# Halving the first batch's query side and writing out the order of every engine in a linear-attention and MLP kernel

## The chip, the core and the metric

The kernel runs on one core of a Trainium2 chip. The metric is device time in microseconds for one execution of the whole program. A core has five engines that run side by side, each through its own list of instructions: PE (matrix products; its weight loads are shown apart as PEld), DVE (vector engine), ACT (scalar engine, which evaluates functions such as exp from a table that has to be loaded), POOL (a second vector engine, which also issues the software DMA queue) and SP (which issues most DMAs). An engine never skips an instruction: one that waits holds up everything behind it on its list.

## What is computed

There are 8 batches, 8 heads, 576 tokens, head size 64 and 128 features. The attention output is the input of a layer norm and a two-layer MLP with a residual.

```python
def phi(x):
    proj = np.einsum('bhsd,df->bhsf', x, w_phi)
    proj = proj - np.max(np.abs(proj), axis=-1, keepdims=True)
    return np.concatenate([np.exp(proj), np.exp(-proj)], axis=-1)
q_p, k_p = (phi(q), phi(k))
kv = np.einsum('bhsf,bhsd->bhfd', k_p, v)
z = np.sum(k_p, axis=2)
num = np.einsum('bhsf,bhfd->bhsd', q_p, kv)
den = np.einsum('bhsf,bhf->bhs', q_p, z)[..., None] + 1e-06
x = num / den                                  # then (batch, token, 512)
mu = np.mean(x, axis=-1, keepdims=True)
var = np.mean((x - mu) ** 2, axis=-1, keepdims=True)
xn = (x - mu) / np.sqrt(var + 1e-06) * g_ln
out = x + np.maximum(xn @ w_ch1, 0.0) @ w_ch2  # 512 x 2048, 2048 x 512
```

## The kernel before

**Units.** Attention is cut into 32 units; a unit is two heads of one batch, 576 tokens each, so that units 0 to 3 are batch 0 and units 4 to 7 batch 1. Of a unit's tokens 512 per head are the main part and 64 the tail; the tails (`px`, L943 and L944) are handled apart. A unit goes through these steps: its q and k are transposed on PE (L829, `qkT_ps`) and copied out as bf16 (`qkT`, L844 on DVE or L846 on ACT). The function `a_main` multiplies by w_phi with tokens on the partitions (`pm`, L984 or L990) and DVE takes the largest absolute value of each token (`m`, L1047, one reduction of 128x1024 for k and one for q). For k, ACT takes the exponentials (`eb`, L1067), a small factor `ek` (L1056, L1060) is folded into v on POOL (`vv`, L1074 to L1080), and PE forms `kv` (L1135, L1141, in the PSUM tile `n_bank`), which is copied out as `KV` (L1149 on DVE, L1151 on ACT). For q, `a_tails` multiplies with features on the partitions (`pt`, L999) and ACT takes the exponentials (`ea`, L1111). `a_num` multiplies `ea` with `KV` on PE (`num`, L1199, L1205), DVE scales and adds the two halves (`numc`, L1221, L1227) and inverts the denominators (`rden`, L1233), and POOL writes the quotient into `x` (L1266, L1270). From unit 4 on, `pm` and `pt` of two units are multiplied together in one group on two halves of the array (`a_group`, 64 rows each).

**Token groups.** The MLP works on groups of four token tiles, 512 tokens. Group 0 is batch 0, so it needs units 0 to 3; group 1 is batch 1. For a group, DVE takes mean and variance (L1338, L1350), the centred `xc` is formed (L1360, L1364), PE transposes it (L1302, `xT_ps`), the copy `xT` (L1312 on DVE, L1314 on ACT) carries g_ln, and then come the two products: `first` (L1431, `hT_ps`, sixteen blocks of four matmuls with 512 columns, each followed by a relu, L1439 on DVE or L1441 on ACT) and `second` (L1463, `ch_ps`). The factor 1/sqrt(var) is applied behind the second product; it is made on ACT as exp(-0.5 ln(var)), with L1370 (Ln) and L1371 (Exp). The last groups use products with fewer multiplications (L1597, L1780 and around).

**Weights.** w_ch1 comes in two DMAs of 1 MB (`load_w1`, L769) and w_ch2 in two (`load_w2`, L787), all issued by POOL through its software queue. Units 8 and later hold their loads back until the second half of w_ch1 has come (`HOLD`).

**The order.** The class `Order` collects every operation with its possible engines, its estimated time, and what it reads and writes. Before the change its `run` is a list scheduler: at each moment an engine takes, among the operations that are ready by its plan, the one with the lowest rank, and ranks come from the tables `OFF`, `SLACK` and `GATE`. The plan fixes the order on each engine (and which engine takes an operation that two could do); the chip then runs these lists and waits on semaphores. Where the plan has PE idle before 75 us (`WARM`), it puts in filler matmuls (L2061 and L2064, `n_bank<-wz`, 128x120), whose result nothing uses.

**The function table of ACT.** Near the start the program calls `preload_act_table_set("natural_log_exp_and_others")` (L1966 before, L2064 after), an operation of ACT with 1.3 us in the plan. The built program shows an ACT_TABLE_LOAD for it, and one ahead of any function that the table then in place doesn't hold.

Of the kernel before, what the change touches and what calls it, by code (L numbers as in the profile page):

```python
# [17 lines left out]
def bcast(ap: bass.AP, dim: int, n: int) -> bass.AP:  # L18
# [7 lines left out]
RELU = -983.1  # L26
WARM = 75.0
COLD, FIRST = 5.6, 10
SLACK = ((0.22, 0.0, 0.0, 1.02), (0.35, 0.6, 1.6, 1.03), (0.22, -1.1, 0.0, 1.28))
HOLD = 1  # L30
SHUT = 0.6
X_DMA, QK_DMA, AHEAD = 1, 8, 3
TILED = 4
LAND, LAND_T, LAND_W, TURN, BARRIER = 2.8, 1.5, 3.0, 0.004, 0.4
MIXED, STUCK = 1.5, 0.3
GATE = (("v", 4), ("v", 5))
OFF = (
    {
        "load": 0.0, "trans": -17.5, "trans.copy": -150.8, "mixed": -0.8, "mixed.max": 0.0,
        "mixed.exp": 45.4, "mixed.fold": 0.0, "k": 7.2, "k.max": -94.2, "k.em": -91.5,  # L40
        "k.exp": -40.2, "en": 0.0, "vv": -43.0, "q": 0.0, "q.max": -8.5, "q.em": 72.1,
        "tails": 0.0, "tails.exp": 121.1, "kv": 56.5, "kv.copy": -218.0, "num0": 940.5,
        "num1": 72.3, "num.dve": -95.7, "g1": 0.0, "g2": 0.0, "g3": 0.0, "put": 7.1, "ln": 0.0,
        "w1": 0.0, "w2": 0.0, "ln.c": 0.0, "ln.t": 0.0, "moe": 0.0,
    },
    {
        "load": 0.0, "trans": 37.9, "trans.copy": 0.9, "mixed": 166.7, "mixed.max": -24.8,
        "mixed.exp": 88.7, "mixed.fold": 0.0, "k": 748.4, "k.max": 0.0, "k.em": -35.7,
        "k.exp": 0.0, "en": 0.0, "vv": -48.0, "q": 0.4, "q.max": -0.3, "q.em": 52.8,
        "tails": 1.6, "tails.exp": 1.2, "kv": 45.2, "kv.copy": 19.6, "num0": -19.2,  # L50
        "num1": 107.5, "num.dve": -989.1, "g1": 0.0, "g2": 0.0, "g3": 0.0, "put": 90.6,
        "ln": 172.1, "w1": 0.0, "w2": 0.0, "ln.c": 0.0, "ln.t": 0.0, "moe": 0.0,
    },
    {
        "load": 0.0, "trans": 94.3, "trans.copy": 0.0, "mixed": 266.0, "mixed.max": -21.1,
        "mixed.exp": -4.0, "mixed.fold": 0.0, "k": -132.9, "k.max": -50.9, "k.em": -145.0,
        "k.exp": -269.5, "en": 0.0, "vv": 0.1, "q": 66.0, "q.max": 2.0, "q.em": 33.6,
        "tails": -201.9, "tails.exp": 120.7, "kv": 8.8, "kv.copy": -27.9, "num0": 5.2,
        "num1": 2.7, "num.dve": 115.4, "g1": 0.0, "g2": 0.0, "g3": 0.0, "put": -58.0, "ln": 0.0,
        "w1": 0.0, "w2": 0.0, "ln.c": 0.0, "ln.t": 0.0, "moe": 0.0,  # L60
    },
    {
        "load": 0.0, "trans": 0.0, "trans.copy": -2.2, "mixed": 27.3, "mixed.max": -46.6,
        "mixed.exp": -1.8, "mixed.fold": 0.0, "k": 11.3, "k.max": -17.6, "k.em": -80.2,
        "k.exp": 0.7, "en": 0.0, "vv": 0.0, "q": -27.7, "q.max": 1.8, "q.em": 0.0,
        "tails": -47.7, "tails.exp": -6.1, "kv": 0.0, "kv.copy": 35.2, "num0": -1.3,
        "num1": 121.1, "num.dve": -1.6, "g1": 0.0, "g2": 0.0, "g3": 0.0, "put": -58.0,
        "ln": -535.9, "w1": 0.0, "w2": 0.0, "ln.c": 34.1, "ln.t": -36.5, "moe": 80.8,
    },
    {  # L70
        "load": 0.0, "trans": 5.5, "trans.copy": 63.5, "mixed": 47.2, "mixed.max": 0.0,
        "mixed.exp": 73.5, "mixed.fold": 0.0, "k": 0.0, "k.max": 0.4, "k.em": -87.0,
        "k.exp": -137.4, "en": 0.0, "vv": 7.8, "q": 0.0, "q.max": 36.3, "q.em": 78.3,
# [417 lines left out]
def kernel(  # L491
# [1612 lines left out]
```

## Time and profile before

| | us |
|---|---|
| median of 3 runs | 357.06 (356.84 to 357.75) |
| span of the profiled execution | 354.4 |
| median less span | 2.7 |
| PE busy | 345.6 (98%) |
| DVE busy | 304.8 (86%) |
| ACT busy | 258.5 (73%) |
| POOL busy | 189.3 (53%) |

The profiled execution's own time is not listed apart from its span; the difference of 2.7 us to the median of the runs is taken as what lies around the span. The page of the profile gives busy time for each engine, groups of instructions by line, and the chain that ended last. In a row of a group, the numbers behind the first bar are total busy us and mean ns of one instruction, and those behind the second bar are the idle time of the engine just ahead of them, with what ended it. In a row of a timeline or of the chain come start, length, engine, operation and count. The view by windows gives the busy time of each engine in a stretch with the number of instructions. Busy time counts overlapping instructions once, so that a mean duration is somewhat longer than what one instruction adds.

### The profile page before, as it was taken

What the parts mean: (1) busy time and instruction counts of PE and PEld (TensorE: products, weight loads), DVE (VectorE), ACT (ScalarE), POOL (GpSimd) and SP (SyncE); (2) the same over time, 40 slices, a digit from 0 to 9 for tenths busy, and PEclk for the clock granted to TensorE, in tenths of its full rate; (3) what the DMA queues carried; (4) which work ended last, traced back from release to release, by engine and by line L of the source; (5) the groups of instructions that cost most, each with busy time, mean ns of one, the idle gap of its engine ahead of it and who ended that gap; (6) DMA issues with size and microseconds to landing.
All of it is one profiled execution on the core that took longest, in us unless ns stands there. A gap on an engine that the chain in (4) does not pass through costs nothing.

```text
span 354.4 us, 9372 instructions
## 1 busy us (share of the span) xinstructions
PE 345.6 (98%) x3606; PEld 221.1 (62%) x3632; DVE 304.8 (86%) x664; ACT 258.5 (73%) x551; POOL 189.3 (53%) x245
## 2 busy tenths in 40 slices
PE   8998999999999999999999999999999999999995
PEld 8987955556554555455545455555555578578884
DVE  5699987899987888988979989897778799999983
ACT  4997988598997996979696975787697833656410
POOL 5499755799644873747478798355546420000000
PEclk9999999999999999999999999999999999999999
DMA  7999999899996888489729242851051005400053
GB/s 210 311 215 287 210 281 246 215 235 258 294 276 175 209 185 215 115 141 280 202 68 209 72 110 47 147 153 35 2 126 63 3 7 116 123 2 3 0 120 118
DMA packets 93676, 53.89 MB, mean 152 GB/s; under 512 B 61104, under 2 KB 88048, under 8 KB 93632
## 3 DMA queue, kind: packets, MB, share of 16 engines
q1 hardware_dynamic: 89392, 47.72, 56.5%
q0 software_dynamic: 3328, 4.49, 7.1%
q10 hardware_dynamic: 912, 1.08, 0.9%
q8 instruction: 28, 0.46, 0.5%
q14 instruction: 16, 0.13, 0.1%
HBM read 36.77 MB, written 9.44 MB: 130 GB/s over the span
## 4 chain that ended last, share of the span: by engine, by line
PE 88%; DVE 8%; ACT 2%; issue 1%; DVEq 0%; ACTq 0%
PE hT_ps L1431 29%; PE ch_ps L1463 22%; PE ch L1597 9%; PE n_bank L2064 4%; PE pm L990 4%; PE n_bank L1141 4%; PE sum L1780 4%; PE num L1199 3%; PE pt L999 2%; DVE m L1047 2%; PE n_bank L1135 1%; DVE numc L1221 1%; PE n_bank L1199 1%; DVE numc L1227 1%; PE n_bank L1205 1%
## 5 line engine op out<-in xcount | busy, mean ns | idle before, releaser
L1431 PE MATMUL hT_ps<-xT,w 128*128 128x512 bf16 x496 | 118.4, 379 | 0.0
L1463 PE MATMUL ch_ps<-w,hT 128*128 128x512 bf16 x362 | 88.9, 379 | 1.3 <-issue 0.3
L1047 DVE TENSOR_REDUCE m<-pm 128x8 f32<-128x1024 f32 x64 | 76.8, 1214 | 7.1 <-PE pm L990 6.5
L1074 POOL TENSOR_TENSOR vv<-v,ek 128x1024 bf16<-128x1024 f32 x32 | 61.1, 1910 | 33.0 <-issue 18.2
L1431 PEld LDWEIGHTS <-w 128*128 128x128 bf16 x496 | 44.2, 98 | 44.0 <-issue 0.8
L1067 ACT ACTIVATE eb<-pm 128x1024 bf16<-128x1024 f32 x64 | 64.5, 1036 | 2.4 <-DVE m L1047 2.3
L1111 ACT ACTIVATE ea<-pt 128x1024 bf16<-128x1024 f32 x64 | 63.8, 1029 | 3.0 <-PE pt L999 2.7
L1266 POOL TENSOR_TENSOR x<-numc,rden 128x128 bf16<-128x128 f32 (+1 forms) x64 | 38.9, 613 | 38.6 <-DVE rden L1233 37.4
L1441 ACT ACTIVATE hT<-hT_ps 128x512 bf16<-128x512 f32 x68 | 40.6, 597 | 24.1 <-PE hT_ps L1431 23.2
L1463 PEld LDWEIGHTS <-hT 128*128 128x128 bf16 x384 | 34.0, 98 | 34.4 <-issue 0.8
L1439 DVE TENSOR_SCALAR hT<-hT_ps 128x512 bf16<-128x512 f32 x56 | 38.5, 687 | 8.6 <-PE hT_ps L1431 8.1
L1199 PEld LDWEIGHTS <-ea 128*128 128x128 bf16 x512 | 24.6, 97 | 10.5 <-issue 1.7
L1141 PE MATMUL n_bank<-vv,eb 128*128 128x65 bf16 x512 | 26.6, 194 | 0.0
L902 POOL TENSOR_TENSOR b<-qk,one 128x1024 bf16<-128x1024 f32 x11 | 20.9, 1896 | 8.9 <-DMA qkT<-b 5.5
L2064 PE MATMUL n_bank<-wz 128*128 128x120 bf16 x347 | 25.0, 224 | 0.1
L1141 PEld LDWEIGHTS <-eb 128*128 128x128 bf16 x512 | 22.3, 98 | 4.3
L1221 DVE TENSOR_TENSOR numc<-num,em 128x390 f32<-128x390 f32 (+1 forms) x40 | 20.3, 513 | 3.3 <-PE num L1199 2.5
L2064 PEld LDWEIGHTS <-wz 128*128 128x128 bf16 x347 | 21.5, 103 | 1.6 <-issue 0.5
L1480 POOL TENSOR_TENSOR o<-o,x 128x512 f32<-128x512 f32 x14 | 16.2, 1154 | 10.5 <-ACT o L1476 10.5
L1338 DVE BATCH_NORM_STATS2 st<-x 128x6 f32<-128x512 bf16 (+1 forms) x40 | 21.3, 569 | 0.4 <-POOL x L1266 0.4
L1199 PE MATMUL num<-KV,ea 128*128 128x65 bf16 x416 | 19.4, 193 | 1.6 <-ACT KV L1151 1.3
L1227 DVE TENSOR_TENSOR numc<-numc,num 128x390 f32<-128x390 f32 (+1 forms) x40 | 20.3, 516 | 0.5
(162 smaller groups left out, 608.7 us busy)
## 6 DMA issues: line engine op xcount, KB each, us to landing
out_dram<-o SPq DMA_DIRECT2D x29, 256.0 KB, 2.6
qk<-in_k_dram SPq DMA_DIRECT2D x12, 512.0 KB, 5.0
qk<-in_q_dram SPq DMA_DIRECT2D x12, 512.0 KB, 6.0
v<-in_v_dram SPq DMA_DIRECT2D x12, 512.0 KB, 4.9
w<-in_moe_w_ch_dram POOLq DMA_DIRECT2D x4, 1024.0 KB, 11.4
qk<-in_k_dram SPq DMA_DIRECT2D x8, 256.0 KB, 6.9
qk<-in_q_dram SPq DMA_DIRECT2D x7, 256.0 KB, 7.5
v<-in_v_dram SPq DMA_DIRECT2D x7, 256.0 KB, 7.4
```

Of the source, the lines that this page charges most:

```text
L1047: nc.vector.reduce_max(out=m, in_=ps, axis=AX.X, apply_absolute_value=True)
L1067: nc.scalar.activation(eb, ps, AF.Exp, scale=(1.0, -1.0)[t])
L1074: eng.tensor_tensor(out=u["vv"][:, :, 0:MX, 0:D], in0=bcast(vb[:, hh, :].rearrange("p (c d) -> p c d", d=D), 1, 2), in1=bcast(e[:, :, 0:MX ...
L1111: nc.scalar.activation(u["EA"][:, t, 0:1024], u["pt"], AF.Exp, scale=(1.0, -1.0)[t])
L1141: nc.tensor.matmul(ps[:, t, c // 4, :], EB[:, t, c, :], vv[:, t, c, :], start=False, stop=(t == 0 and c == MX - 1), skip_group_check=True,)
L1199: nc.tensor.matmul(ps[t][:, i, :], ea(u, t, c), KV[:, t, c // 4, :], start=True, stop=True,)
L1266: eng.tensor_tensor(out=dst, in0=src, in1=by, op=ALU.mult)
L1431: nc.tensor.matmul(st["ps"], w1_sb[:, kc, jj * P : (jj + 1) * P], xT_bufs[g % XB][:, kc::KC, :], start=(kc == 0), stop=(kc == KC - 1),)
L1439: nc.vector.tensor_relu(h_sb, st["ps"])
L1441: nc.scalar.activation(h_sb, st["ps"], AF.Relu)
L1463: nc.tensor.matmul(ch[g, i], hT[g, jj][:, i * P : (i + 1) * P], w2_sb[:, jj, :], start=(jj == 0), stop=(jj == JC - 1),)
L2064: nc.tensor.matmul(warm, wz, wz[:, 0:WN], start=False, stop=False, skip_group_check=True)
```

## The change

It has four parts.

1. **Halves.** For units 0 to 3 (`HALVED = 4`) the q side is worked in two halves of 256 tokens per head. `q_half` does four matmuls for both layouts into one PSUM tile (`qh`, L887 and L889 after), one reduction of 128x4 (over 128x512 elements, L892), one small exponential (L902) and two exponentials of 128x512 (L906); `num_half` takes the place of `a_num` (its DVE lines are L949, L954 and L957, its POOL lines L978 and L986), with its intermediate results in the buffers `xT1` and `xT2`; `x_trans_half` (L1348, copies on L1359 or L1361) and `first_half` (eight matmuls of 256 columns, L1379, and one relu, L1391 or L1393) do the same for group 0's MLP, sixteen blocks for 2 x 8. Mean, variance and 1/sqrt(var) of group 0 are made for each half (Ln on L1458, Exp on L1459). The first half of group 0 thus needs only the first 256 tokens of units 0 to 3.
2. **First loads and clears.** The first loads stay in their order. The clears of `ea1` and `vx1` on DVE stand ahead of the two casts of w_phi into `wbk` instead of behind them.
3. **A written-out list.** `run` no longer chooses: a table `ORDER` holds, for each engine, the numbers of its operations in the order in which it takes them. `SLACK`, `LAG`, `TOOK` and the durations in the plan are new numbers, which now decide only where the plan has PE idle, hence where fillers go. `GATE` lets the two halves of w_ch1 start behind the v of units 2 and 3 instead of 4 and 5, and w_ch2 no longer waits for the first half of w_ch1 in the plan.
4. **What the list says.** Some operations stand elsewhere or on another engine than before.

The core of the diff:

```diff
-GATE = (("v", 4), ("v", 5))
+GATE = (("v", 2), ("v", 3))
+ORDER = {
...
+    "ACT": """
+        2 14 24 99 100 84 85 80 83 98 93 94 95 107 108 120 121 106 125 126 183 119 103 166 167
...
     def run(self):
-        waiting, free, room, events, done = {}, {}, self.room, [], []
+        turn = {engine: [int(n) for n in text.split()] for engine, text in ORDER.items()}
...
+                elif place[engine] < len(turn[engine]):
+                    op = self.ops[turn[engine][place[engine]]]
...
-    for i in range(2):
-        rows = slice(i * D, (i + 1) * D)
-        nc.vector.tensor_copy(out=wbk[rows, i, :], in_=wphi_f[rows, :])
     ea_bufs = []
...
     clear_vx(vx_bufs[1])
+    for i in range(2):
+        rows = slice(i * D, (i + 1) * D)
+        nc.vector.tensor_copy(out=wbk[rows, i, :], in_=wphi_f[rows, :])
...
-        dma("POOL", V, 1 << 21, emit, r=[("w1 came", 0)],
+        dma("POOL", V, 1 << 21, emit,
             w=[*(("w2", n * NW // ND + i) for i in range(NW // ND)), ("w2 came", n)], us=0.78, row=2048)
...
+    def q_half(u, h):
+            for a in range(2):
+                nc.tensor.matmul(ps[:, 0, a], x[:, a, :], wbk, start=True, stop=True)
+            for i in range(2):
+                nc.tensor.matmul(ps[:, 1, i], wbk[:, i, :], x, start=True, stop=True)
...
+    def first_half(h, j2):
+            for k in range(2):
+                jj = 2 * j2 + k
+                for kc in range(KC):
+                    nc.tensor.matmul(
+                        st["ps"][:, k].rearrange("p (i t) -> p i t", t=P),
+                        w1_sb[:, kc, jj * P : (jj + 1) * P],
+                        xT_bufs[0][:, kc::KC, :][:, 2 * h : 2 * h + 2, :],
+                        start=(kc == 0), stop=(kc == KC - 1),
+                    )
...
-        def rstd():
-            nc.scalar.activation(rstd_x[:, g, :], mv_x[:, g, :, 1], AF.Ln, bias=eps_sb)
-            nc.scalar.activation(rstd_x[:, g, :], rstd_x[:, g, :], AF.Exp, scale=-0.5)
+        def rstd(at=slice(0, NM)):
+            nc.scalar.activation(rstd_x[:, g, at], mv_x[:, g, at, 1], AF.Ln, bias=eps_sb)
+            nc.scalar.activation(rstd_x[:, g, at], rstd_x[:, g, at], AF.Exp, scale=-0.5)
...
+        scale = ("rstd", g) if g else ("rstd", 0, i // 2)
         add("PE", mm(n, DM), turn_of(g + 1), products,
-            r=[("rstd", g)] + [hkey[g, jj] for jj in js]
+            r=[scale] + [hkey[g, jj] for jj in js]
+            + [("hTh", jj, i // 2) for jj in js if g == 0]
...
-            a_main(u, 0)
+            for half in range(2):
+                q_half(u, half)
...
+                (num_half if halved(n - 1) else a_num)(units[n - 1], part)
```

What the lists say at the places that matter, from the built programs. On ACT, the start of the list before holds the table load of the call at L1966, ahead of all work (`qkT0` is unit 0's transposed copy):

```order
L564 DMA wphi_f_82<-in_w_phi_dram 64x128
L676 DMA qk0_100<-in_q_dram 128x2x256
L676 DMA v0_101<-in_v_dram 128x2x256
L1966 ACT_TABLE_LOAD
L846 COPY qkT0_141<-qkT_ps_204 128x512 x2
L1067 ACTIVATE eb0_148<-pm_228 128x1024 x2
L1111 ACTIVATE ea0_125<-pt_300 128x1024
```

It is the only table load in the program before. Group 0's 1/sqrt(var) (L1370, L1371) stands between exponentials, with no load beside it:

```order
L1360 ACTIVATE xc0_136<-x_156,mv_154 128x512 x2
L1056 ACTIVATE ek_1130<-m2_119 128x12
L1060 ACTIVATE ek_1130<-m2_119 128x12
L1067 ACTIVATE eb1_149<-pm_1015 128x2x4x128
L1370 ACTIVATE rstd_155<-mv_154,eps_111 128x4
L1371 ACTIVATE rstd_155<-rstd_155 128x4
```

After the change there is a load at the start of ACT's list too (ahead of the first L906), and five more. Two of them stand around the Ln of the first half's 1/sqrt(var), between relus of `first_half` (L1393):

```order
L1393 ACTIVATE hT_151<-hT_ps_1166 128x2x256
L1393 ACTIVATE hT_151<-hT_ps_1180 128x2x256
L1458 ACT_TABLE_LOAD
L1458 ACTIVATE rstd_155<-mv_154,eps_111 128x2
L1459 ACT_TABLE_LOAD
L1459 ACTIVATE rstd_155<-rstd_155 128x2
L1393 ACTIVATE hT_151<-hT_ps_1221 128x2x256
L1086 ACTIVATE eb0_148<-pm_1200 128x2x4x128
L794 CAST b16_0_145<-qk1_102 128x1024
```

The other three stand around the second half's 1/sqrt(var), the last of them being the call that stood at L1966 before and now is L2064 (`pm_1505` is a product of a later unit that waits for its exponentials, `KV` the copy of a finished kv):

```order
L1170 CAST KV_1578<-n_bank_150 128x260
L1458 ACT_TABLE_LOAD
L1458 ACTIVATE rstd_155<-mv_154,eps_111 128x2
L1459 ACT_TABLE_LOAD
L1459 ACTIVATE rstd_155<-rstd_155 128x2
L794 CAST b16_2_147<-qk2_104 128x1024
L2064 ACT_TABLE_LOAD
L1075 ACTIVATE ek_1634<-m2_119 128x12
L1079 ACTIVATE ek_1634<-m2_119 128x12
L1086 ACTIVATE eb0_148<-pm_1505 128x2x4x128 x2
```

So the call went from the front of ACT's list to behind both of group 0's Ln, and each of these Ln and Exp got a load of its own; no load stands behind it in the program.

On POOL, the two DMAs of w_ch2 (L787) stood side by side before:

```order
L769 DMA w1_132<-in_moe_w_ch1_dram 128x4x1024
L1266 TENSOR_TENSOR x_156<-numc_785,rden_807 128x128
L1270 TENSOR_TENSOR xs_134<-numc_785,rden_807 128x64
L1266 TENSOR_TENSOR x_156<-numc_735,rden_775 128x2x3x64
L787 DMA w2_133<-in_moe_w_ch2_dram 128x8x512 x2
L1074 TENSOR_TENSOR vv_909<-v2_105,ek_895 128x2x8x64
L1079 CAST vv_909<-ek_895 128x2x8
L1080 TENSOR_TENSOR vv_909<-vx1_107,ek_895 128x2x130
```

After, the first of them (L680) stands just ahead of these rows, and the second behind two units' `vv`:

```order
L978 TENSOR_TENSOR x_156<-xT2_140 128x2x2x64 x2
L1093 TENSOR_TENSOR vv_1014<-v2_105,ek_972 128x2x8x64
L1098 CAST vv_1014<-ek_972 128x2x8
L1099 TENSOR_TENSOR vv_1014<-vx1_107,ek_972 128x2x130
L1452 TENSOR_TENSOR xc0_136<-mv_154,x_156 128x512
L1093 TENSOR_TENSOR vv_1162<-v2_105,ek_1158 128x2x8x64
L1098 CAST vv_1162<-ek_1158 128x2x8
L1099 TENSOR_TENSOR vv_1162<-vx1_107,ek_1158 128x2x130
L680 DMA w2_133<-in_moe_w_ch2_dram 128x8x512
```

The second half of w_ch2 thus moved behind `vv_1162`, which waits for `ek_1158`, made while the first half's products run.

On PE, the program before holds 348 filler matmuls, 346 of them ahead of group 0's first product; after there are 269, 253 of them ahead of it and 16 behind, in pieces of 5 and 11. The matmuls of the MLP, of the kv and of the num are as many as before, except that group 0's first product is 128 matmuls of 256 columns instead of 64 of 512.

More of the change, by code (lines that the diff above doesn't have):

```diff
@@ L393, in run @@
                 if kind == 1:
[L394 to L404 removed]
+                    offered.add(op.number)
@@ L418, in run @@
-                for item in passed:
-                    heapq.heappush(queue, item)
+                if engine in loads:
+                    if loads[engine]:
+                        op = self.ops[heapq.heappop(loads[engine])[1]]
+                elif place[engine] < len(turn[engine]):
+                    op = self.ops[turn[engine][place[engine]]]
+                    if op.number not in offered or (
+                        op.acquire and room[op.acquire[0]] < op.acquire[1]
+                    ):
+                        op = None
+                    else:
+                        place[engine] += 1
@@ L442, in run @@
                         both = 1000.0
-                    if engine == "DMA" and both > 0 and lag > 0:
+                    if engine == "DMA" and both > 0 and lag > 2.0:
                         lag += MIXED
@@ L452, in run @@
                     first, last = port[0], port[1]
-                    us = us.us + max(0.0, first - now if now < first else last - now)
-                    if now < last and any(not item[2].engine for item in waiting["POOL"]):
+                    us = us.us + max(0.0, (first if now < first else last) - now - 0.15)
+                    n = place["POOL"]
+                    if now < last and n < len(turn["POOL"]) and turn["POOL"][n] in offered:
                         us += STUCK
@@ L480, in run @@
                         offer(o)
-        assert not any(op.left or not op.engine for op in self.ops)
+        assert all(place[engine] == len(turn[engine]) for engine in turn)
         for op in done:
@@ L747, in load_tails @@
                 queue, rank, dst, src, [(key + "x" + str(half), j)], 16384 * TG,
-                row=4096 if queue == "POOL" else 256, hold=HOLD >= 0 and H <= n < 2 * H, n=n,
+                row=256, hold=HOLD >= 0 and H <= n < 2 * H, took=TOOK.get((key, n, half)),
             )
@@ L1886, in moe @@
         done = 0
+        if g == 0:
+            for h in range(2):
+                for j2 in range(JC // 2):
+                    first_half(h, j2)
+            return
         if g == FAST[0]:
@@ L1926, in rk @@
     def rk(stage, n):
[L1927 removed]
+        return ()
     units, pairs = [], []
```

664 lines of the change are left out of this document (298 added, 366 removed), and 117 rows, old and new, of tables (OFF, ORDER, TOOK).

## The prediction

> **What bounds the kernel now.** I read the page first.
>
> ```profile
> span 354.4 us, 9372 instructions
> PE 345.6 (98%) x3606; PEld 221.1 (62%) x3632; DVE 304.8 (86%) x664; ACT 258.5 (73%) x551; POOL 189.3 (53%) x245
> ...
> L1067 ACT ACTIVATE eb<-pm 128x1024 bf16<-128x1024 f32 x64 | 64.5, 1036 | 2.4 <-DVE m L1047 2.3
> ...
> L1441 ACT ACTIVATE hT<-hT_ps 128x512 bf16<-128x512 f32 x68 | 40.6, 597 | 24.1 <-PE hT_ps L1431 23.2
> ```
>
> PE is busy for 98% of the span, but a filler counts as busy. So I split the span at 44.6 us, where group 0's first MLP product starts. Columns: window, its length, busy time (and count) of PE, PEld, DVE, ACT, POOL, then PE's clock, DMA share, GB/s.
>
> ```profile
> 16.10:44.60 28.50, 26.23 (x508) 23.82 (x508) 28.00 (x69) 25.89 (x62) 24.39 (x35) 1.00 1.18 243
> 44.60:75.00 30.40, 30.24 (x282) 16.53 (x284) 25.55 (x50) 23.43 (x53) 19.53 (x26) 1.00 1.16 234
> 75.00:345.00 270.00, 268.50 (x2550) 161.67 (x2568) 238.29 (x514) 198.53 (x418) 138.27 (x171) 1.00 0.53 129
> ```
>
> Up to the first product DVE has 28.00 of 28.50 us of work and bounds; PE fills up with dummies. Behind it PE is the bound, without room: 30.24 of 30.40 and 268.50 of 270. So the time is PE's useful work, plus fillers, plus PE's waits, plus a tail of DVE and a store that don't change. Pieces of the chain that ended last (start, length, what) show the prices on PE:
>
> ```profile
> 1.28 2.80 PE n_bank L2064 x28
> 4.08 0.43 PE qkT_ps L829 x4
> ...
> 40.72 1.57 PE n_bank L2064 x30
> 42.29 0.67 PE xT_ps L1302 x12
> ...
> 44.59 0.86 PE hT_ps L1431 x4
> ...
> 64.18 0.37 PE num L1199 x12
> ...
> 66.97 0.55 PE pm L990 x16
> ...
> 75.44 0.26 PE n_bank L1141 x8
> ...
> 77.46 0.33 PE pm L990 x8
> ```
>
> A filler is 1.57/30 = 0.052 us (cold, at the start, 2.80/28 = 0.100), a 512-column matmul 0.86/4 = 0.215, a kv matmul 0.26/8 = 0.033, one of num 0.37/12 = 0.031.
>
> The sum is made against the profiled execution, 354.4; its distance of 2.7 us to the median of the runs, 357.06, I carry over unchanged. About 0.3%, 1.1 us, is what a measurement here can tell from no change.
>
> **The change part by part.**
>
> *Fillers ahead of the first product.* What lets the product come earlier is DVE's shorter list, which these rows price (by shape, up to 44.6 us; then one of the timeline):
>
> ```profile
> L1047 DVE TENSOR_REDUCE m<-pm 128x8 f32<-128x1024 f32 x13 | 15.7, 1214 | 0.5 <-PE pm L984 0.5
> L1338 DVE BATCH_NORM_STATS2 st<-x 128x6 f32<-128x256 bf16 x8 | 2.9, 408 | 0.0
> L1221 DVE TENSOR_TENSOR numc<-num,em 128x390 f32<-128x390 f32 x5 | 2.7, 546 | 0.0
> ...
> 42.55 1.27 DVE L1312 TENSOR_SCALAR xT<-xT_ps,ngln 128x512 bf16<-128x512 bf16 x3
> ```
>
> From the first KV copy to the last `xT` copy ahead of the product, eight large reductions become three and four halves (estimate 0.6 each, half of 1.214): about 3.7 us. Eight statistics become four: 1.4. The `num` arithmetic of four units instead of five: about 1.6. Copies, small reductions, `xT` in halves (1.27 to about half): about 1.2. Together some 7.9 us, an estimate. The first product would then start near 36.7 instead of 44.59. Of that, about 3.4 us are work that now lies behind the product instead of ahead (two blocks of kv at 18 x 0.033, num, eight transposes at 0.67/12, two groups of products), which PE does in any case. The rest, 4.5, must be fillers, and the count in the built program says the same: 346 ahead before, 253 after, 93 fewer. Of these 18 are cold ones at the start, ahead of the first transposes, which need k:
>
> ```profile
> 0.74 0.45 SPq L676 DMA_DIRECT2D qk<-in_k_dram  x1
> ```
> ```profile
> qk<-in_k_dram SPq DMA_DIRECT2D x1, 256.0 KB, 2.8
> ```
>
> k lands at 0.74 + 2.8 = 3.54, and the transposes start at 4.08, so the cold ones can give back 0.54 at most. The other 75 give 75 x 0.052 = 3.9. Together -4.5 (bounds 0, if idle replaces them all, to 3.9 + 18 x 0.100 = -5.7).
>
> *Fillers behind it.* 16 instead of 2: 14 x 0.052 = +0.7.
>
> *Paired 64-row products.* Stretches of them fall from 46 to 42; two apart cost 2 x 0.33 for 16 matmuls, one together 0.55, so 0.11 for each switch: -0.4.
>
> *Blocks of 256 columns.* 128 at half of 0.215 instead of 64 at 0.215: nothing by that price, +0.1 for their starts.
>
> *The second half waits for DVE.* Behind the first half's products (with other work 6.5 us on PE) DVE has four statistics, two large reductions, three relus, a KV copy and the `xT` copies: about 7.6 us. +0.9, bounds 0 to 1.5.
>
> *ACT's function tables.* Rows of ACT's timeline, and one cast by shape:
>
> ```profile
> 2.47 1.28 ACT L1966 ACT_TABLE_LOAD   x1 [2.47 <-issue]
> 4.54 0.58 ACT L846 COPY qkT<-qkT_ps 128x512 bf16<-128x512 bf16 x1 [0.78 <-PE qkT_ps L829]
> ...
> 31.17 0.41 ACT L1151 CAST KV<-n_bank 128x260 bf16<-128x260 f32 x1
> ...
> 42.21 0.35 ACT L1370 ACTIVATE rstd<-mv,eps 128x4 f32<-128x4 f32 x1
> 42.59 0.21 ACT L1371 ACTIVATE rstd<-rstd 128x4 f32<-128x4 f32 x1
> ```
> ```profile
> L900 ACT CAST b<-qk 128x1024 bf16<-128x1024 f32 x1 | 1.0, 1037 | 0.0
> ```
>
> Before, the one load stands at 2.47, where ACT has nothing to do, and Ln and Exp at 42.21 need none. After, five loads of 1.28 us stand amid the MLP. First pair (around the first half's Ln): ACT has a relu of about 0.6, Ln 0.35, Exp 0.21, 2 x 1.28 and the next relu, 4.3 us in all. PE meanwhile, from the product whose relu stands ahead of the pair to the one that needs the buffer of the relu behind it, has 8 num (0.25), 16 pm (0.55), a block (0.86), 12 num (0.37) and 18 kv (0.6) = 2.7. Without loads ACT needs under 2.3 there, so 0.4 is spare; with them PE waits about 1.6. Second place: PE has 25 products of 0.215, 20 num, 5 fillers and a small one, 6.4 us, until a product needs the buffer that two exponentials set free; ACT has KV 0.41, Ln and Exp 0.56, the cast 1.04, the moved call's load 1.28, two small ones 0.2, two exponentials 1.94 = 5.4. The spare is 1.0, the two loads ask 2.56: +1.6. Together +3.2; bounds 0 (all hidden by later spare) to 5 x 1.28 = +6.4.
>
> [...]
>
> *Two clears ahead of the casts.* The casts wait for w_phi's load anyway: nothing, and some 0.8 us at most if DVE came late, which the first transposes' copies would show.
>
> Sum: -4.5 + 0.7 - 0.4 + 0.1 + 0.9 + 3.2 = 0.0. Span 354.4, time 357.1: no change that can be measured. The gain in front is given back at ACT.
>
> **The rivals.**
>
> *Faster: the loads hide.* ACT is busy 23.43 of 30.40 us from 44.6 to 75, and waits 24.1 us in all for PE ahead of the L1441 relus. If its lists have slack where I see little (0.4 and 1.0), the +3.2 fall away: 357.1 - 3.2 = 353.9, and 353.0 without the second half's wait too. Against it: the relu frees one of only three buffers, so a stop of 2.6 us passes on to PE within two blocks.
>
> *Slower: w_ch2 comes late.* The second DMA of w_ch2 moved on POOL's queue:
>
> ```profile
> L787 POOL DMA_DIRECT2D w<-in_moe_w_ch_dram x2: 895/906/918, 30.5 to 31.4; - x2
> ...
> DMA to landing us min/median/max: 12.8/15.6/18.3
> ```
> ```profile
> 47.27 1.91 POOL L1074 TENSOR_TENSOR vv<-v,ek 128x1024 bf16<-128x1024 f32 x1 [1.65 <-ACT ek L1060]
> 49.12 0.25 POOL L1079 CAST vv<-ek 128x16 bf16<-128x16 f32 x1
> 49.27 0.62 POOL L1080 TENSOR_TENSOR vv<-vx,ek 128x260 bf16<-128x260 f32 x1
> ```
>
> It was issued by 31.4 and stands now behind the `vv` of a unit whose reduction comes behind the first half's products: 36.7 + 6.5 + 0.9 + 1.2 + 0.2 = 45.5, and a `vv` of 2.6: issue at 48.1. PE comes to the product that reads it at about 36.7 + 19.8 (its list up to there) + 0.9 + 1.6 = 59.0. It decides from a landing time of 10.9 us on: at 12.8 PE waits 1.9, at 18.3 it waits 7.4: 359.0 to 364.5. For it speaks that both measured landings are longer; against it that these two were issued one behind the other and shared the queue, so that one alone should take less than 12.8.
>
> *Slower: a switch costs more than its load.* Behind the load at 2.47 to 3.75 ACT's next instruction starts at 4.54; up to 0.78 us of that could belong to the load. For the five loads, 5 x 0.78 = +3.9: 361.0. The row puts it down to PE instead.
>
> *The change does not do what it says.* If another engine than DVE holds the first product, idle replaces the fillers: 357.1 + 4.5 = 361.6. Against it: POOL and ACT have shorter lists ahead of it too.
>
> **How the numbers follow.** My forecast has 0.36 (own range 355.5 to 358.7, from the bounds of the waits), the hidden loads 0.33, late w_ch2 0.15, dearer switches 0.10, no earlier product 0.06. The forecast's own range is spread 0.07 faster, 0.21 within 0.3%, 0.08 slower; with the rivals faster is 0.07 + 0.33 = 0.40, same 0.21, slower 0.08 + 0.15 + 0.10 + 0.06 = 0.39. The range goes from 352.0 (loads and the second half's wait hidden, and some of the cold fillers gained too) to 362.0 (dearer switches and an idle front; a part of the late w_ch2 lies above it, some 0.07).
>
> **What would show it.** Right: the first L1379 product near 36.7; DVE still the fullest engine ahead of it; five table loads of 1.28 us on ACT between there and 75 us; PE idle behind them, about 1.6 us each time, with ACT as the releaser; 269 fillers. Hidden loads: the same loads, and no idle time on PE. Late w_ch2: PE idle ahead of a `ch_ps` product with a DMA as the releaser. Dearer switches: gaps on ACT beside the loads. It would be wrong in its base if the first product started later than 40, or if PE waited somewhere that no list named here leads to.

## The result and the profile after

| | before | after |
|---|---|---|
| median, us | 356.95 (356.76 to 357.75, 4 runs) | 360.88 (360.6 to 363.8, 4 runs) |
| span of the profiled execution, us | 354.4 | 358.8 |

The ratio is 1.0127, with a 95% interval of 1.0086 to 1.0167: the changed kernel is slower by 1.3%, 3.9 us in the median and 4.4 in the spans. The forecast was 357.1, no change; its range, 352.0 to 362.0, holds the time.

The page of the changed kernel begins and groups as follows.

```profile
span 358.8 us, 9335 instructions
PE 345.7 (96%) x3625; PEld 224.8 (63%) x3625; DVE 301.1 (84%) x676; ACT 259.2 (72%) x562; POOL 180.0 (50%) x243
...
L1379 PE MATMUL hT_ps<-xT,w 128*128 128x256 bf16 x128 | 15.3, 273 | 2.6 <-ACT hT L1393 1.7
```

PE is busy for as long as before (345.7, before 345.6) in a span that is 4.4 us longer. So PE now waits, and the windows say where (the same three stretches as in the prediction; PE's busy time comes first behind the length):

```profile
16.10:44.60 28.50, 25.64 (x445) 23.16 (x442) 26.22 (x65) 24.64 (x68) 19.80 (x29) 1.00 0.98 211
44.60:75.00 30.40, 28.65 (x369) 20.98 (x367) 24.84 (x53) 28.95 (x56) 16.69 (x24) 1.00 1.10 229
75.00:345.00 270.00, 268.24 (x2564) 159.55 (x2563) 232.64 (x511) 198.40 (x425) 137.01 (x177) 1.00 0.59 133
```

From 44.6 to 75 us PE was busy for 30.24 us before and now for 28.65, while ACT went from 23.43 to 28.95, nearly the whole stretch. Who PE waited for (total us, times, longest):

```profile
PE hT_ps L1379 <- ACT hT L1393: 1.7, 1, 1.7
PE qkT_ps L722 <- POOL ident masks.py:199: 1.6, 1, 1.6
PE pm L1009 <- ACT eb L1086: 1.2, 1, 1.2
PE num L938 <- ACT ea L906: 1.0, 2, 0.7
...
PE hT_ps L1379 <- DMA w<-in_moe_w_ch_dram: 0.8, 1, 0.8
```

The same view of before has one wait above a microsecond that isn't the fixed one of 1.0 for `wz` at the start:

```profile
PE num L1199 <- ACT KV L1151: 1.3, 1, 1.3
```

The first and the third wait of after belong to the function tables. ACT's timeline at the first place:

```profile
50.68 1.11 ACT L1393 ACTIVATE hT<-hT_ps 128x512 bf16<-128x512 f32 x2
51.81 1.28 ACT L1458 ACT_TABLE_LOAD   x1
53.10 0.29 ACT L1458 ACTIVATE rstd<-mv,eps 128x2 f32<-128x2 f32 x1
53.42 1.28 ACT L1459 ACT_TABLE_LOAD   x1
54.71 0.20 ACT L1459 ACTIVATE rstd<-rstd 128x2 f32<-128x2 f32 x1
54.82 0.58 ACT L1393 ACTIVATE hT<-hT_ps 128x512 bf16<-128x512 f32 x1
```

and what PE shows for both places, with its wait for `w_ch1` between (the bracket is the idle time before the row):

```profile
41.38 1.05 PE L1379 MATMUL hT_ps<-xT,w 128*128 128x256 bf16 x8 [0.83 <-DMA w<-in_moe_w_ch_dram]
...
55.45 2.78 PE L1379 MATMUL hT_ps<-xT,w 128*128 128x256 bf16 x24 [1.75 <-ACT hT L1393]
...
77.30 0.40 PE L1009 MATMUL pm<-wbk,qkT 64*128 64x128 bf16 x8 [1.19 <-ACT eb L1086]
```

The relu at 54.82 had to stand behind two loads, so the products at 55.45 started 1.75 us late. At the second place three more loads (69.77, 71.38 and 73.82 on ACT) end in a wait of 1.19.

The whole, summed from PE's records (each matmul counted up to the start of the next one, gaps over 0.07 us as idle):

| us | before | after |
|---|---|---|
| first L1431 or L1379 product starts | 44.6 | 38.65 |
| fillers | 20.1 (348) | 16.6 (269) |
| idle | 2.2 | 7.9 |
| other work | 327.2 | 329.2 |
| PE ends | 350.6 | 354.6 |
| behind it | 3.8 | 4.2 |

The product came 5.9 us earlier and the fillers gave back 3.6. Idle time took 5.7, and the useful work itself grew by 2.0.

### The profile page after: what moved, and what is told of

Read it like the earlier page. It is cut to its first block, busy times and chain, and to the rows that moved or that the text cites. A ratio compares the mean times of both kernels' runs of the same rounds, so it can differ in the third digit from the quotient of the medians.

```text
span 358.8 us, 9335 instructions
## 1 busy us (share of the span) xinstructions
PE 345.7 (96%) x3625; PEld 224.8 (63%) x3625; DVE 301.1 (84%) x676; ACT 259.2 (72%) x562; POOL 180.0 (50%) x243
## 4 chain that ended last, share of the span: by engine, by line
PE 78%; ACT 8%; DVE 6%; DMA 4%; issue 2%; POOL 1%; SPq 1%; ACTq 0%; POOLq 0%; DVEq 0%
PE hT_ps L1522 26%; PE ch_ps L1554 18%; PE ch L1690 10%; PE n_bank L1160 3%; PE pm L1009 3%; PE sum L1873 3%; DMA w<-in_moe_w_ch_dram 3%; PE n_bank L2164 2%; PE num L1218 2%; PE pt L1018 2%; ACT ea L1130 2%; DMA qk<-in_q_dram 1%; ACT eb L1086 1%; PE hT_ps L1379 1%; ACT ea L906 1%
## 5 line engine op out<-in xcount | busy, mean ns | idle before, releaser
L1522 PE MATMUL hT_ps<-xT,w 128*128 128x512 bf16 x432 | 103.6, 379 | 0.0
L1086 ACT ACTIVATE eb<-pm 128x1024 bf16<-128x1024 f32 x64 | 64.2, 1042 | 12.8 <-DVE m L1066 12.8
L1522 PEld LDWEIGHTS <-w 128*128 128x128 bf16 x432 | 38.6, 98 | 38.9 <-issue 1.3
L1130 ACT ACTIVATE ea<-pt 128x1024 bf16<-128x1024 f32 x56 | 55.3, 1034 | 7.2 <-PE pt L1018 7.0
L1285 POOL TENSOR_TENSOR x<-numc,rden 128x128 bf16<-128x128 f32 (+1 forms) x56 | 33.6, 611 | 38.1 <-DVE rden L1252 37.8
L1530 DVE TENSOR_SCALAR hT<-hT_ps 128x512 bf16<-128x512 f32 x40 | 26.7, 679 | 2.6 <-PE hT_ps L1522 2.4
L1009 PE MATMUL pm<-wbk,qkT 64*128 64x128 bf16 x448 | 19.7, 217 | 1.2 <-ACT eb L1086 1.2
L1009 PEld LDWEIGHTS <-qkT 64*128 64x128 bf16 x448 | 13.8, 94 | 10.1 <-issue 7.9
L1099 POOL TENSOR_TENSOR vv<-vx,ek 128x260 bf16<-128x260 f32 x32 | 19.9, 621 | 0.0
L2164 PE MATMUL n_bank<-wz 128*128 128x120 bf16 x268 | 19.2, 229 | 0.2 <-ACT ea L854 0.2
L1379 PE MATMUL hT_ps<-xT,w 128*128 128x256 bf16 x128 | 15.3, 273 | 2.6 <-ACT hT L1393 1.7
```

The source lines that it names most:

```text
L1009: nc.tensor.matmul(ps[:, half * 4 + c, :], u["qkT"][rows, cols], wbk[rows, half, :], start=True, stop=True,)
L1086: nc.scalar.activation(eb, ps, AF.Exp, scale=(1.0, -1.0)[t])
L1130: nc.scalar.activation(u["EA"][:, t, 0:1024], u["pt"], AF.Exp, scale=(1.0, -1.0)[t])
L1285: eng.tensor_tensor(out=dst, in0=src, in1=by, op=ALU.mult)
L1522: nc.tensor.matmul(st["ps"], w1_sb[:, kc, jj * P : (jj + 1) * P], xT_bufs[g % XB][:, kc::KC, :], start=(kc == 0), stop=(kc == KC - 1),)
L2164: nc.tensor.matmul(warm, wz, wz[:, 0:WN], start=False, stop=False, skip_group_check=True)
```

## The experiments

The theory: the five table loads cost PE about 2.9 us; the rest is a front that gives 2 us less than forecast, since PE stops for 1.55 us at the start and stays slow for longer, and then waits for w_ch1. The rival: the loads only fill time in which something else, mostly a weight, would have held PE, and what the front gains can't be kept. Numbers in the lists are those of `ORDER`; in kernels with a written count of fillers ahead of each operation (the same counts that the plan gave, "fixed fillers") line numbers are 13 higher. Times are medians with range and number of runs, ratios are to the kernel before, which took 356.8 to 356.9 beside them.

**1. The call for the table at the start.** Operation 26 is the preload. It moves to ACT's idle time at the start; the rest is unchanged, PE's list included, and one load is left.

```diff
-        2 14 24 99 100 84 85 ...          (ACT)
+        2 14 24 26 99 100 84 85 ...
-        ... 323 505 26 495 ...
+        ... 323 505 495 ...
```

> The call that loads ACT's table stands at the front of ACT's list again; PE's list is the same to the last filler, and one table load is left in the program. Theory A (the five loads amid the MLP cost what PE visibly waited beside them, 1.75 us behind the first pair and 1.19 us behind the other three): both waits go, 360.9 - 2.9 = 358.0, 357.5 to 358.6. Rival B (ACT has slack and PE would have waited there for something else, a buffer or DVE): 360 or more, with another releaser in the same places. [...]

Measured 359.5 (357.24 to 363.7, 12 runs), 1.007 [1.0042, 1.0098]. The profiled execution has a span of 356.3, 2.5 less than after. On ACT's timeline the first pair now runs without loads:

```profile
50.31 1.11 ACT L1393 ACTIVATE hT<-hT_ps 128x512 bf16<-128x512 f32 x2
51.26 0.34 ACT L1458 ACTIVATE rstd<-mv,eps 128x2 f32<-128x2 f32 x1
51.63 0.20 ACT L1459 ACTIVATE rstd<-rstd 128x2 f32<-128x2 f32 x1
52.37 0.60 ACT L1393 ACTIVATE hT<-hT_ps 128x512 bf16<-128x512 f32 x1 [0.53 <-PE hT_ps L1379]
```

The relu ends at 52.97 instead of 55.40, and waits for PE, not PE for it. Both of PE's waits for the tables are gone, and one that was hidden shows:

```profile
PE ch_ps L1554 <- DMA w<-in_moe_w_ch_dram: 0.7, 1, 0.7
```

That is the second product's wait for w_ch2. The profiled execution bears out the theory (2.5 of 2.9). The median gained only 1.4, which leaves it above the 357.5 to 358.6 of theory A, and its interval overlaps that of after: seven runs took 357.2 to 359.5 at a mean clock of 0.997 or more, and five took 361.2 to 363.7 at 0.988 to 0.995. In the profiled executions a mean clock of 0.994 or 0.995 goes with a fall of the granted clock to 0.50 to 0.54 in one window of 2 us and 0.61 to 0.83 in the next (kernels 5, 6, 7 and 9 below); after, with 0.998, shows 1.00 in every such window up to 356 us. So the five probably had such a fall. What set it off in them stays open.

**2. More fillers ahead of the first transposes.** `COLD, FIRST = 5.6, 10` becomes `5.6, 25`, so that PE doesn't stop at the start.

> 25 instead of 10 fillers at the very start, so that PE has no pause before the first transposes; everything else as in the changed kernel. Theory A (PE came to speed only near 9.3 us instead of near 4.7, because it paused from 2.27 to 3.83, and that made 29 fillers and the first products twice as long, so that the first MLP product came 2 us late): speed by about 5 us, the first reductions 1.3 to 2 us earlier, the first MLP product near 37, and 1 to 2 us less in all, 359 to 360. Rival B (the front hangs on the loads of q and w_phi or on ACT's list, so the faster clock only makes idle time): within 0.4 us of 360.9.

Measured 360.67 (359.65 to 362.48, 4 runs), 1.011 [1.0081, 1.0139]; span 357.9, 0.9 less. By the medians rival B holds: 360.67 can't be told from the 360.88 of after. In the profiled executions, which the following is read from, the front behaves as theory A has it. PE's start in after, and then in this kernel:

```profile
1.07 1.20 PE L2164 MATMUL n_bank<-wz 128*128 128x120 bf16 x10
3.83 0.59 PE L722 MATMUL qkT_ps<-ident,qk 128*128 128x128 bf16 x4 [1.55 <-POOL ident masks.py:199]
4.20 2.31 PE L2164 MATMUL n_bank<-wz 128*128 128x120 bf16 x21
...
6.73 1.06 PE L1003 MATMUL pm<-wbk,qkT 128*128 128x256 bf16 x4
```
```profile
1.07 2.71 PE L2164 MATMUL n_bank<-wz 128*128 128x120 bf16 x25
3.83 0.38 PE L722 MATMUL qkT_ps<-ident,qk 128*128 128x128 bf16 x4
4.05 1.27 PE L2164 MATMUL n_bank<-wz 128*128 128x120 bf16 x21
...
6.17 0.60 PE L1003 MATMUL pm<-wbk,qkT 128*128 128x256 bf16 x4
```

With the pause, 21 fillers take 2.31 us, without it 1.27. The first product starts at 37.05 instead of 38.65. But the next one that needs the second half of w_ch1 waits 1.47 instead of 0.83. The profile puts this wait down to ACT's relu, which ends at 40.42; but in after the same product starts at 41.38 while the two relus ahead of it still run (40.88 to 42.02), so it doesn't need them, and w_ch1's DMA, issued at 30.70 and landed 9.7 later, fits its start at 40.43. The kernels below show more of the start: at half speed a filler takes 0.10 (the prediction's 2.80/28), at full speed 0.052, and the moment at which PE comes to full speed differs between executions of one list. With 10 fillers and the pause it came at about 9.1, 8.3, 9.0, 6.5 and 8.2 us (after, kernels 1, 3, 9, 10) and the first product at 38.65, 38.61, 38.40, 37.43 and 38.23; with 25 fillers at about 3.8, 5.4, 7.0, 7.0 and 5.6 (kernels 2, 4, 5, 11, 12), and the product at 37.05, 37.88, 37.85, 37.81 and 37.22. (Kernels 6 to 8 are left out, since they delay the product in another way.) So the pause costs the first product some 0.7 us in the mean (38.26 against 37.56), and the 1.6 of this pair of executions is partly chance.

**3. The k side first.** On ACT's list k's two exponentials (L1086) stand ahead of the first half's two of q (L906): `99 100 84 85` becomes `84 85 99 100`.

> Unit 0's two large exponentials of k stand ahead of the two of q's first half on ACT, as they did in the kernel before; nothing else moves. Theory A (the first KV copy came at 18.5 instead of 16.1 partly because k's exponentials wait behind q's, which themselves wait for DVE's reduction): KV copy 1.5 to 2 us earlier, first MLP product up to 1.5 us earlier, 359.5 to 360.5. Rival B (from the first KV on, DVE's list is the limit and had slack to catch up, or the second kv needs the later parts anyway): first product within 0.3 us of 38.65 and no change in all.

Measured 360.16 (359.69 to 361.06, 4 runs), 1.0093 [1.0072, 1.0113]. The first product starts at 38.40, 0.25 earlier: the order of the two on ACT isn't what delays it, and the rival held.

**4. All three.** Call early, 25 fillers, and w_ch1's second DMA (155) earlier on POOL's list:

```diff
-        ... 131 219 206 205 33 200 155 241 ...   (POOL)
+        ... 131 219 155 206 205 33 200 241 ...
```

> The table call at the front, 25 fillers at the start, and the second half of w_ch1 issued by POOL behind the fourth vv instead of three operations later (the plan then puts 10 more fillers ahead of the first MLP product and as many fewer behind). Theory A (table waits 2.9, cold start 1 to 2, the wait of 0.83 for w_ch1's second half, added up): 360.9 - 4.7 to 5.7 = 355.2 to 356.2, below the kernel before. Rival B (the waits cover each other, and DVE or ACT's list is what is left): 357.5 or more.

Measured 356.93 (355.88 to 358.34, 12 runs), 1.0002 [0.9987, 1.0018]: the kernel before is reached again, not beaten, and the time lies between the two that were expected. What is left of PE's waits:

```profile
PE xT_ps L1321 <- DVE xc L1443: 1.1, 1, 1.1
...
PE hT_ps L1379 <- DMA w<-in_moe_w_ch_dram: 0.8, 1, 0.8
...
PE ch_ps L1554 <- DMA w<-in_moe_w_ch_dram: 0.5, 1, 0.5
```

Issuing w_ch1 3.2 us earlier left its wait as it was (0.77, after 0.83): it took 11.4 us to land instead of 9.0, so it came 0.8 earlier, and PE came to it 0.8 earlier too.

**5. w_ch2 earlier too.** As 4, with w_ch2's second DMA (174) earlier on POOL's list, and fixed fillers.

```diff
-        ... 288 169 246 293 274 322 309 174 444 ...   (POOL)
+        ... 288 169 174 246 293 274 322 309 444 ...
```

> As the kernel of the three edits (table call at the front, 25 fillers at the start, second half of w_ch1 behind the fourth vv), with the fillers at the places where the changed kernel has them, and the second half of w_ch2 issued right behind the first instead of behind two units' vv. Theory A (its place on POOL's list is all that makes w_ch2 late): PE's wait of 0.5 us for it at the second product goes, w_ch1's wait stays near 0.8: 356.0 to 356.6. Rival B (the software queue or the shared DMA engines are full, and an earlier issue only moves the wait to q, k, v or w_ch1): a wait for a DMA of at least 0.5 us stands elsewhere, 356.9 or more.

Measured 359.89 (358.04 to 360.91, 4 runs), 1.0082 [1.0054, 1.011]. The wait for w_ch2 is gone and a larger one has come. PE's list of waits has it first, and ACT's timeline says why:

```profile
PE hT_ps L1392 <- ACT hT L1406: 2.4, 1, 2.4
```
```profile
52.34 1.02 ACT L1099 ACTIVATE eb<-pm 128x1024 bf16<-128x1024 f32 x1
56.37 1.04 ACT L807 CAST b<-qk 128x1024 bf16<-128x1024 f32 x1 [3.01 <-DMA qx<-in_k_dram]
57.32 0.59 ACT L1406 ACTIVATE hT<-hT_ps 128x512 bf16<-128x512 f32 x1
```

A cast of the next unit's k waits for its load, and the relu stands behind it. The 512 KB load of q that is issued between 36 and 58 us took 8.9 us to land in kernel 4, and 14.0 here. And PE loses time after the wait as well (windows; the number behind POOL's count is PE's clock):

```profile
58.00:60.00 2.00, 2.00 (x11) 1.02 (x12) 0.30 (x1) 1.69 (x7) 2.00 (x4) 0.54 0.01 4
60.00:62.00 2.00, 1.78 (x14) 0.98 (x12) 1.90 (x3) 1.75 (x3) 2.00 (x3) 0.61 0.16 34
62.00:64.00 2.00, 2.00 (x19) 1.11 (x18) 0.78 (x3) 1.55 (x5) 1.54 (x4) 1.00 0.94 158
```

For 4 us the granted clock is 0.54 and then 0.61, some 1.7 us of work lost. The rival held here: with this weight moved forward, the load of q took 5.1 us longer to land, and the 512 KB load of k issued in that stretch took 9.4, where the median of two was 5.9 in kernel 4.

**6. The first half of w_ch1 earlier still.** As 5, with `150` behind `109`.

> As before, and the first half of w_ch1 issued behind the second vv instead of the third, where POOL waits 1.5 us for DVE anyway. Theory A (the second half lands about 5 us behind the first because they share a queue, so it is the first that has to go earlier): no wait for w_ch1 at the first product's fourth block, 0.8 us less, 355.2 to 355.8. Rival B (the loads of k, q and v of units 4 to 7 then share the DMA engines with w_ch1 earlier, and the attention ahead of the first product comes late): the first MLP product 0.5 us or more later than 37.9, 356.5 or more.

Measured 360.11 (359.65 to 363.97, 6 runs), 1.0115 [1.008, 1.015]. The transposes now wait 0.82 for k and 1.14 for q near 31 us, the granted clock falls to 0.82, 0.50 and 0.83 from 32 to 38 us, and the first product starts at 40.65. The same exchange, in the front.

**7. The list that each step had suggested.** As 6, with DVE's two `xc` (544, 546) given to ACT ahead of `553 500`, and no fillers behind the first product.

> As before, and two centred tiles of group 1 are made by ACT instead of DVE (where two of them took 2.36 us instead of 0.72 when POOL's vv ran beside), and the 16 fillers behind the first MLP product are left out. Theory A (PE's last wait, 1.08 us ahead of group 1's transposes, is DVE held up by POOL's vv; the fillers behind the product are plain loss): 1.1 + 0.8 less than the kernel of the expectation ahead of this one, 353.3 to 354.2, faster than the kernel before by 0.8% or so. Rival B (PE then waits for what comes next: the POOL chain of x, mean and variance for group 1): 355 or more.

Measured 359.71 (359.23 to 360.9, 6 runs), 1.0086 [1.0067, 1.0104], against some 354 expected: a miss. It keeps the late loads of 5 and 6: PE waits 2.34 for a relu and 1.4 for a q load.

**8. The same with the call back at its late place**, so that the loads are priced once more, in another list.

> The kernel of the expectation ahead of this one, with the table call back where the change put it, so that the five loads stand amid the MLP again; nothing else differs. Theory A (they cost PE what it waited beside them, 1.75 + 1.19): 2.5 to 3.0 us more than that kernel, with PE's waits for ACT in the same two places. Rival B (what they cost depends on the other waits, which were late enough there to cover a part): 3.5 us or more, since nothing covers them now; or 1.5 or less, if the waits for weights had been the cause.

Measured 362.76 (361.63 to 363.24, 4 runs), 1.0164 [1.0143, 1.0184], 3.05 more than kernel 7. PE waits 1.75 for the relu and 1.46 ahead of `pm` at the second place. This is the theory's price, but in medians alone (of six and four runs, whose ranges don't overlap): the spans of the two profiled executions, 359.1 and 359.9, lie only 0.7 apart, since that of kernel 7 has a wait of 2.34 at the first place in any case and a fall of the clock behind it (0.50 from 60 to 62 us), and that of kernel 8 has none.

**9. The call in the middle.** In after's list, `26` moves to right behind the first half's Exp; nothing else in the lists changes, but the plan then puts 11 fewer fillers behind the first product.

```diff
-        276 308 363 361 318 355 403 ...   (ACT)
+        276 308 363 361 318 26 355 403 ...
-        ... 323 505 26 495 ...
+        ... 323 505 495 ...
```

> The changed kernel with the table call right behind the first half's Exp: three loads stand at the first place instead of two, none at the second, and the plan puts 11 fewer fillers behind the first product. Theory A (PE's wait at the first place grows by one load to 3.0 us, and a pause of PE longer than about 2 us halves its granted clock for some 4 us, as in the two profiles where waits of 2.36 and 2.34 us were followed by 0.50 to 0.61): 1.28 - 1.19 - 0.58 + 1.9 = 1.4 us more, 362 to 363, with a clock near 0.5 between 57 and 62 us. Rival B (the low clock there had another cause, such as chance): the same wait of 3.0 us, the clock stays at 1.00, 360.2 to 360.6.

Measured 363.56 (362.57 to 366.34, 4 runs), 1.0198 [1.0158, 1.0239], in the way that the theory had it and somewhat more than its 362 to 363. Three loads now stand together at the first place, and PE's wait grows from 1.75 to 3.18, after which the clock falls:

```profile
56.77 4.33 PE L1379 MATMUL hT_ps<-xT,w 128*128 128x256 bf16 x24 [3.18 <-ACT hT L1393]
```
```profile
58.00:60.00 2.00, 2.00 (x11) 1.42 (x10) 1.75 (x3) 1.14 (x3) 0.17 (x1) 0.50 1.46 160
60.00:62.00 2.00, 2.00 (x16) 1.55 (x13) 0.58 (x2) 1.06 (x3) 0.12 (x1) 0.70 0.97 193
```

**10. Call early and the cast later.** As 1, with ACT's cast (449) behind `353 404`, fixed fillers, to see whether the cast makes kernel 1's spread.

> The kernel with only the table call at the front, and on ACT the cast of the k and q of a unit held back until w_ch1 has come (L794, three rows behind the first half's Exp) now behind the next relu and exponential. Theory A (the times of that kernel spread from 357.2 to 363.7 because this cast waits for a load whose landing varies, the relu behind it frees PE's buffer, and a pause of over 2 us also halves the clock): all runs between 357 and 359, clock 0.997 or more. Rival B (the spread comes from the cold start or from chance): some runs at 361 to 363 with a clock of 0.995 as before.

Measured 359.02 (358.32 to 362.24, 9 runs), 1.0068 [1.0043, 1.0094]. One run of nine is above 361, where it was five of twelve: fewer, but too few runs to show it. That all runs would stay below 359 did not come true.

**11. The best of the parts.** As 4, with the cast of 10, `xc` on ACT and no fillers behind the product; w_ch2 as in after.

> The three edits (table call at the front, 25 fillers at the start, second half of w_ch1 behind the fourth vv), that cast behind the next relu and exponential, two centred tiles of group 1 on ACT instead of DVE, and no fillers behind the first product; w_ch2 stays where the change put it. Theory A (what was left of the three edits' kernel was DVE's wait for POOL of 1.08 us and 0.32 us of fillers): 356.9 - 1.4 = 355.5, 355.0 to 356.0, faster than the kernel before by about 0.4%. Rival B (POOL's chain of x, mean and variance for group 1 ends last there): 356.5 or more.

Measured 356.55 (355.63 to 358.17, 12 runs), 0.9991 [0.9975, 1.0007]: not to be told from before, and above the 355.0 to 356.0 of theory A. Not POOL's chain, as rival B had it, but the weights took back what it gained:

```profile
PE hT_ps L1392 <- DMA w<-in_moe_w_ch_dram: 1.5, 1, 1.5
...
PE ch_ps L1567 <- DMA w<-in_moe_w_ch_dram: 1.0, 1, 1.0
```

**12. The same with w_ch2 one place earlier** (`274 174 322 309`).

> As before, and the second half of w_ch2 issued ahead of one unit's vv and a centring on POOL, some 6 us earlier, instead of behind them. Theory A (with the cast out of the way, w_ch2's earlier transfer costs nothing and PE's 0.5 us wait for it goes): 0.5 us less than the kernel of the expectation ahead of this one. Rival B (it takes transfer time from the held loads of k, q and v, which come late for the units after them): 0.5 us more or worse, with a wait for a DMA on ACT or POOL.

Measured 357.89 (357.01 to 359.63, 12 runs), 1.0031 [1.0014, 1.0048]: by its time, the rival. PE's wait for w_ch1 is 0.9, and it waits 0.8 for a `vv` on POOL; no view shows whether a load came late for it.

**Together.** In ten profiles, the first product that needs w_ch1's second half starts between 40.1 and 42.0 us, while the first product of all lies between 37.05 and 38.65; the earliest (37.05) gives 40.43, and one of 37.43 gives 41.27. So part of what the front gains turns into a wait there (the profile names w_ch1's DMA in eight of the ten; in kernels 1 and 2 it names ACT, but the load of that weight on PE, under PEld, waits 0.8 and 1.7 for the same DMA). In kernels 5 and 6, where w_ch2 or both weights are issued sooner, loads of q or k come later (14.0 us to land instead of 8.9 in kernel 5, waits of 0.82 and 1.14 in kernel 6); for kernel 12 only the longer time is shown.

## Why the prediction was right and wrong

The forecast of no change failed: 360.88 lies outside the range of the forecast alone (355.5 to 358.7). Only the wide range that takes in the rivals holds it, and its upper end came from two of them, dearer switches and an idle front, of which the first is out and the second came true in part. Each term of the sum beside its measure, in us:

| term | forecast | measured |
|---|---|---|
| fillers ahead and behind | -4.5 + 0.7 | -3.6 |
| idle at the start in their place | 0 | +1.55 |
| first products at half speed | 0 | +0.9 |
| 64-row pairs | -0.4 | 0 |
| 256-column blocks | +0.1 | +0.6 |
| second half waits for DVE | +0.9 | 0 |
| second half of w_ch1 late | not in the sum | +0.83 |
| table loads | +3.2 | +2.9 |
| the rest (0.4 of it behind PE's end) | 0 | +1.2 |
| sum | 0.0 | +4.4 |

**The table loads were right**, in mechanism, place and size: five loads, 1.75 and 1.19 us on PE against 1.6 and 1.6, with ACT as the releaser. Moving the call took 2.5 off the span and 1.4 off the median, and moving it back in another list cost 3.05 in medians. The first rival, that they hide, is out.

**The front was wrong.** The step that failed is "*Fillers ahead of the first product*", with "the cold ones can give back 0.54 at most". It counted 18 fewer fillers at the start as nearly free, but took the work behind them at its old speed. With 10 fillers PE has nothing from 2.3 to 3.83 us, where `ident` comes, and then runs at half speed to about 9.1 us instead of 4.7: four `pm` matmuls take 1.06 from start to end instead of 0.60. So 1.55 us of filler became idle time, and useful work grew by 0.9. Kernel 2 took both away.

The forecast had the first product at 36.7, and it came at 38.65. The stretch that DVE's shorter list was to shorten, from the first KV copy to this product, came out as priced (before, then after; DVE's busy time is the third behind the length):

```profile
16.12:44.59 28.47, 26.20 (x508) 23.80 (x508) 27.99 (x69) 25.86 (x62) 24.38 (x35) 1.00 1.18 243
18.54:38.65 20.11, 18.08 (x349) 16.81 (x348) 18.98 (x50) 17.64 (x53) 14.18 (x21) 1.00 0.98 223
```

It is 8.4 us shorter, where 7.9 were forecast, with 9.0 us less work on DVE, which is still the fullest engine. But the forecast let the stretch begin at 16.1 as before, and the first KV copy now comes at 18.54. That step, what lies ahead of the first KV copy, was put at nothing. In kernel 2 the copy comes at 16.96 and the product again 20.1 us behind it. So of the 2.4 us, 1.6 go with the slow start in this pair of executions; the other 0.8 lie in what the new lists do ahead of the copy, and which part of them no run shows (the order of kernel 3 moved the copy by 0.2).

**The blocks of 256 columns cost a little more than half.** Half of a 512-column matmul, 0.1075, was assumed. Where many stand together, that is nearly so:

```profile
46.38 4.54 PE L1379 MATMUL hT_ps<-xT,w 128*128 128x256 bf16 x40
50.76 0.23 PE L1218 MATMUL num<-KV,ea 128*128 128x65 bf16 x2
```

The 40 take 4.38 us up to the next row, 0.1095 each. Over all 128, counted from start to start, it is 14.4 us beside 13.8 for the 64 before: +0.6.

**The 64-row pairs gave nothing.** The prediction counted 46 stretches of them before and 42 after; PE's records show 42 in both kernels, and the 504 matmuls take 23.2 us before and 23.3 after.

**"The second half waits for DVE"** didn't happen; PE waited ahead of it for w_ch1, whose second half had been issued at 32.3 and landed 9.0 us later. The prediction looked for a late weight only at w_ch2, and took w_ch1 as there; by its own words a wait to which no list that it names leads makes its base wrong. Of w_ch2 it was right that a wait may come: none in after (issued at 51.5, 3.4 later than forecast, but landed 9.1 later, less than the 10.9 that decides), and 0.5 to 1.0 us in kernels 1, 4, 10 and 11, where PE came earlier.

**Dearer switches** are out: behind each load the next instruction starts within 0.01 to 0.03 us (51.81 + 1.28 = 53.09, Ln at 53.10). Ahead of it the relus end at 51.79 and the load starts at 51.81. At the other four loads (53.42, 69.77, 71.38 and 73.82) the gaps on both sides are 0.01 to 0.03 too, where the rival had put up to 0.78.

So the change lost because its loads cost what the sum said, while its front paid some 2.6 us less than the sum said (idle time and slow products in the place of fillers), and 0.8 at w_ch1 and 0.5 in the smaller blocks came on top; the 0.9 for DVE's wait was not spent. Not settled: what makes the last 0.8 us ahead of the first KV copy, what the rest of 1.2 consists of, and why executions of kernel 1 spread by 6 us.

## What to carry to other kernels

Price a shorter stage by what sets the pace next: here it was the weights' DMAs (waits of 0.4 to 1.9 us for w_ch1), and where they were moved forward (kernels 5 and 6) loads that the shorter stage lives from came later. Fillers at the start of PE's list were not waste here that could be taken away one for one; ask what the real products cost at the speed that PE then has (1.06 us instead of 0.60 for four `pm` matmuls). And when an order is written out by hand, look where one-time instructions such as the call for a function table have come to stand: moved to idle time, this one gave back 2.5 us of span in one list and, in medians, 1.4 and 3 us in two.

## What the runs showed of the hardware

**PE's clock fell behind waits of 2.34, 2.36 and 3.18 us, and once behind two shorter ones.** These three (kernels 7, 5 and 9) were followed by 4 us with a granted clock of 0.50 and 0.71, 0.54 and 0.61, and 0.50 and 0.70, in windows of 2 us. Behind two waits of 0.82 and 1.14 that end at 31.07 and 32.62 us in kernel 6 it was 0.82, 0.50 and 0.83 from 32 to 38 us. It stayed at 1.00 behind the wait of 1.75 in after (windows from 56 to 62 us), and kernel 10, with a wait of 1.87, has a mean clock of 0.999. In kernel 8 PE waited 0.5 for a k load and 1.2 for a q load, and the clock is 1.00 from 28 to 38 us, where PE is busy for only 1.14 and 1.21 of 2 us from 30 to 32 and from 32 to 34. What decides it, no run shows.

**The moment of full speed differed between executions of one list.** Five executions whose PE lists begin alike reached it between 6.5 and 9.1 us, with PE busy from 3.83 on (in kernel 1 with a gap of 0.56); five others, busy from 1.0 on, between 3.8 and 7.0. That is a spread of 2.6 and 3.2 us from first to last. The column of the granted clock shows 1.00 in these stretches; the slow start is read only from the time of the fillers.

**DVE beside POOL.** In kernel 4 two `xc` of DVE took 2.36 us while a `vv` of POOL ran from 77.65 to 79.60; in after two of the same shape took 0.72, beside the end of another POOL operation (`o`, until 81.08) and without a `vv`. PE's wait of 1.1 for `xc` in kernel 4 comes right behind. PE waits 1.1 for `xc` in kernel 9 as well and 0.6 in kernels 1, 5, 6 and 10; in after and in kernels 2 and 3 its list of waits has none. That the `vv` is the cause, no run shows by itself. The rows of DVE and POOL in kernel 4, and of DVE in after:

```profile
77.38 2.36 DVE L1443 TENSOR_SCALAR xc<-x,mv 128x512 bf16<-128x512 bf16 x2
```
```profile
77.65 1.95 POOL L1093 TENSOR_TENSOR vv<-v,ek 128x1024 bf16<-128x1024 f32 x1
```
```profile
80.78 0.72 DVE L1443 TENSOR_SCALAR xc<-x,mv 128x512 bf16<-128x512 bf16 x2
```
